# Three weight bits by way of ScalarE, and fewer idle products ahead of the first batch

## The chip, the cores and the metric

One Trainium2 chip, one of its cores. The metric is the time of one execution on the device in microseconds, as the median of several runs. The engines of the core are PE (TensorE, the matmuls), DVE (VectorE), ACT (ScalarE), POOL (GpSimd) and SP (SyncE, which issues most transfers); 16 DMA engines move data between the memory and the core.

## The reference, cut to what matters

Windowed causal attention with a distance bias over 8 batches of 8 heads, 576 positions and 64 dimensions, and behind it a network with a maximum of three linear maps.

```python
scores = scale * np.matmul(q, k.transpose(0, 1, 3, 2))
...
mask = (rel >= 0) & (rel < window)          # window = 128
scores = np.where(mask, scores + bias[None], -1000000000.0)
...
attn = attn / (np.sum(attn, axis=-1, keepdims=True) + 1e-09)
return np.matmul(attn, v).astype(np.float32)
...
x = np.ascontiguousarray(attn_out.transpose(0, 2, 1, 3)).reshape(B * S, H * D)
...
h = np.maximum(np.maximum(x @ w1, x @ w2), x @ w3)     # x 4608 x 512, w 512 x 768
return (h @ w_out).astype(np.float32)                  # w_out 768 x 512
```

The four weight matrices come as float64. The kernel takes them as 64-bit words and makes the float32 words on the chip.

## The kernel before, in words

**Layout.** The attention runs in steps: a task is a batch and a pair of heads, and a step is one block of 128 query rows of a task (five blocks, the last of 64 rows). A step has score products on PE (L563), a select and a bias with a row minimum on DVE, the exponential on ACT with its sum, a normalisation, transposes on PE (L671), masks on POOL (L700, L704) and the mixing with V on PE (L727, L759, later L782). The network's products go in units of six or nine matmuls of 128 x 288: those of the first batch by `plain_unit` (L1072), those of the other seven batches by `unit` and `multiply` (L1173), with fewer products per unit by a Strassen-like scheme. The attention of batch b+1 stands between the units of batch b.

**Weights.** `preparing` walks the 12 weight groups in `A_ORDER`. For each, `fetch` issues two loads of 512 KB (float64 halves, L138), `convert` turns each half into float32 words (24 calls in all), and `part` splits these into a high and a low fp32r part: a copy on ACT, then a subtraction on DVE (`halve`), for group after group of tiles `wt`, `ow`, `hs`, `xs`. The float32 words also go out to memory (L157) for the sums of the second batch, and the split parts to `keep` (L308, L295).

**Convert.** A float64 is a low word `lw` and a high word `hw`. The float32 word is sign and top exponent bit of `hw`, then 29 further bits of `hw` moved up by three, then the three top bits of `lw`. Three DVE instructions over 128 x 512 words do it: L146 moves and masks `hw` into a scratch tile `xt` (one buffer), L149 moves `lw` down by 29 and joins it into `xt`, L154 joins the top two bits of `hw` and writes the result over the first half of the loaded tile.

**Products that nothing reads.** `busy` puts bf16 matmuls of 128 x 512 on PE (L501), out of a constant tile into a PSUM bank that nobody reads; each is tied behind the matmul before it. `BUSY` holds how many follow what: eight at the start, eight after each of the first two score calls (`next`), five after each later score call (`s`), two after each transposing call (`t`), none after mixing (`x`). `plain_x(0)`, the split of the first batch's first half, ends this for good. The trace holds 73 weight loads of L501: 8, 16, 7 x 5 and 7 x 2.

**Order.** Up to the end of the first batch's units (`fix`) the framework's scheduler lays out each engine's order when the program is compiled, so an edit can reorder that part. Behind `fix`, PE, DVE and ACT keep the order that the kernel's own planner wrote (`job`, `issue`, `reach`). Each engine executes its instructions in order; the DMA queue of SP too.

Of the kernel before, what the change touches and what calls it, by code (L numbers as in the profile page):

```python
# [10 lines left out]
I32 = mybir.dt.int32  # L11
BF16 = mybir.dt.bfloat16
U32 = mybir.dt.uint32
AF = mybir.ActivationFunctionType
ALU = mybir.AluOpType
PSUM = bass.MemoryType.PSUM
# [2 lines left out]
LOAD_I = 1  # L19
LAG_T, LAG_X, LAG_X0 = 4, 6, 6  # L20
FOLLOW = 64
BUSY = {'start': 8, 'next': 8, 's': 5, 't': 2, 'x': 0}
GROUPS = (1, 4)
SHIFT = (0, 2, 4)
O_PACE = 0.285
# [5 lines left out]
def attention_maxout_kernel(  # L31
# [11 lines left out]
    nc = tc.nc  # L43
# [36 lines left out]
    nc.vector.memset(warm, 0.0)  # L80
    nc.scalar.activation(warm, warm, AF.Exp)
    ident = const.tile([P, P], F32, name="ident")
# [4 lines left out]
        out=prev, in_=prev, pattern=[[1, P]], compare_op=ALU.is_gt, fill=0.0,  # L87
# [3 lines left out]
    bias = const.tile([P, H, P], mybir.dt.bfloat16, name="bias")  # L91
# [5 lines left out]
    def slopes(hp):  # L97
        for h in (2 * hp, 2 * hp + 1):
            nc.scalar.activation(bias[:, h, :], dist, AF.Copy, scale=-8.0 * 2.0 ** (-8.0 * (h + 1) / H))
        nc.gpsimd.affine_select(  # L100
# [25 lines left out]
    raws = {}  # L126
# [11 lines left out]
            nc.sync.dma_start(raws[g, j], w_all[g, j].bitcast(I32))  # L138

    def convert(g, j):  # L140
        both = raws[g, j].bitcast(U32).rearrange("p (n w) -> p n w", w=2)
        lw, hw = both[:, :, 0], both[:, :, 1]


        u = xk_p.tile([P, 2, C], F32, name="xt").rearrange("p a c -> p (a c)")[:, :DM].bitcast(U32)
        nc.vector.tensor_scalar(  # L146
            out=u, in0=hw, scalar1=3, scalar2=0x3FFFFFFF, op0=ALU.logical_shift_left, op1=ALU.bitwise_and
        )
        nc.vector.scalar_tensor_tensor(  # L149
            out=u, in0=lw, scalar=29, in1=u, op0=ALU.logical_shift_right, op1=ALU.bitwise_or  # L150
        )

        out = raws[g, j][:, :DM]
        nc.vector.scalar_tensor_tensor(  # L154
            out=out.bitcast(U32), in0=hw, scalar=0xC0000000, in1=u, op0=ALU.bitwise_and, op1=ALU.bitwise_or
        )
        nc.sync.dma_start(  # L157
            w32[g][:, 1:3] if j else w32[g][:, ::3], out.bitcast(F32).rearrange("p (i w) -> p i w", w=W),
        )
# [47 lines left out]
    def job(engine, ns, slack, what, r=(), w=()):  # L207
        if not fixed:
            what()
            return  # L210
        j = Job(engine, ns, clock["pe"] + slack, what, r, w)
        for k in w:
            wrote[k] = j
        for k in r:
            read.setdefault(k, []).append(j)
        jobs.append(j)
# [210 lines left out]
    def preparing():  # L427
        fetch(A_ORDER[0])
        fetch(A_ORDER[1])
        for n, g in enumerate(A_ORDER):  # L430
            for j in range(2):
                convert(g, j)
                yield
            while AHEAD <= g < 9 and (g - 3 if AHEAD == 3 else g % 3, "plain") not in used:
                yield True
            for c in range(2):
                part(g, c)
                yield
            if n + 2 < 5:
                fetch(A_ORDER[n + 2])  # L440
            elif n + 2 == 5:
                for x in range(5, 5 + 4-1):
                    fetch(A_ORDER[x])
            elif n + 4 < NG:
                fetch(A_ORDER[n + 4])
# [50 lines left out]
    def busy(what):  # L496
        if idle[0] == "over":
            return
        ps = ps_m.tile([P, 512], F32, name="ps_m2")
        for _ in range(BUSY[what]):  # L500
            ins = nc.tensor.matmul(  # L501
# [87 lines left out]
    def score(t, i):  # L589
# [35 lines left out]
        def exponential(j):  # L625
            act.activation(
                p[:n, j], shifted[j][:n], AF.Exp, bias=st[:n, 0, h, j:j + 1], scale=-1.0,
                accum_out=st[:n, 1, h, j:j + 1],
# [20 lines left out]
    def normalise(t, i):  # L649
        n = rows[i]  # L650
        st, two = stats[t, i]
        for a, p in enumerate(two):
# [5 lines left out]
            for j in range(2):  # L658
                job("act", 293, 6000, partial(
                    act.activation, p[:n, j], p[:n, j], AF.Copy, scale=st[:n, 2, a, j:j + 1],  # L660
                ), r=[("st", t, i)], w=[("p", t, i - len(two) + 1 + a, j)])
# [546 lines left out]
    for t, (b, hp) in enumerate(tasks):  # L1208
        for i in range(NB):
            s = place_of[t, i] + shift[b]  # L1210
# [31 lines left out]
            g = next(e for e in GROUPS if e >= i)  # L1242
# [92 lines left out]
```

## Time and profile before

| what | before |
| --- | --- |
| runs | 747.1, 749.12, 747.11 us, median 747.11 |
| profiled execution | 748.33 us, of which 746.6 us are the span from the first to the last instruction |
| instructions | 20349 |
| PE busy | 738.4 us (99%) |
| DVE busy | 559.3 us (75%) |
| ACT busy | 496.0 us (66%) |
| POOL busy | 169.7 us (23%) |
| mean granted clock of PE | 0.999 |

Busy times overlap between engines. The ends of matmuls are modelled, so PE counts as busy in short waits too. 1.7 us of the profiled execution lie outside the span, and it took 1.22 us more than the median.

### The profile page before, as it was taken

How to read it: one execution, taken by the hardware profiler on the slowest of the kernel's cores; microseconds unless marked ns; L12 is line 12 of the kernel's file. 1: busy time of each engine (PE TensorE's matmuls, PEld its weight loads, DVE VectorE, ACT ScalarE, POOL GpSimd, SP SyncE). 2: the span in 40 equal slices, each digit the busy share in tenths (PEclk: the TensorE clock that was granted, in tenths of full speed). 3: DMA queues.
4: the chain of work that ended last, by engine and by line, in shares of the span. 5: the costliest groups of instructions: out<-in, count | busy, mean ns of one | idle time of the engine just before them, and what ended most of it. 6: DMA issues, size and time to landing. Idle time of an engine off the chain costs nothing.

```text
span 746.6 us, 20349 instructions
## 1 busy us (share of the span) xinstructions
PE 738.4 (99%) x7468; PEld 681.1 (91%) x7473; DVE 559.3 (75%) x1921; ACT 496.0 (66%) x1698; POOL 169.7 (23%) x371
## 2 busy tenths in 40 slices
PE   9999999999999999999999999999999999999998
PEld 4487888999999999999999999999999999999998
DVE  6989998959999477866679476684777756683663
ACT  5776886868887677665677676585776756552332
POOL 2431222012132232212322122221322123301100
PEclk9999999999999999999999999999999999999999
DMA  8799986969985688837896488856888379985631
GB/s 293 263 311 317 327 278 203 311 214 316 368 280 192 216 294 299 269 121 241 309 307 223 147 270 304 276 180 217 283 303 277 121 234 310 299 311 177 233 118 64
DMA packets 59091, 188.10 MB, mean 252 GB/s; under 512 B 6256, under 2 KB 21616, under 8 KB 52336
## 3 DMA queue, kind: packets, MB, share of 16 engines
q0 software_dynamic: 14976, 95.43, 38.8%
q1 hardware_dynamic: 43872, 91.31, 35.8%
q8 instruction: 59, 0.97, 0.5%
q14 instruction: 40, 0.33, 0.2%
q10 hardware_dynamic: 144, 0.07, 0.0%
HBM read 154.53 MB, written 32.24 MB: 250 GB/s over the span
## 4 chain that ended last, share of the span: by engine, by line
PE 86%; DVE 8%; DMA 3%; ACT 2%; issue 1%; SPq 0%; POOL 0%; DVEq 0%; ACTq 0%; POOLq 0%
PE ps_m L1173 57%; PE ps_m L1072 6%; PE ps_s L563 6%; PE pt L671 6%; PE ps_x L782 5%; PE ps_m L501 2%; DVE hq L174 1%; DMA keep<-wt 1%; PE pt L1173 1%; DVE wt L174 1%; ACT p L174 1%; DVE hs L174 1%; PE ps_x L759 1%; DMA hs<-in_w_all 1%; DMA wt<-keep 1%
## 5 line engine op out<-in xcount | busy, mean ns | idle before, releaser
L1173 PE MATMUL ps_m<-xs,wt 128*128 128x288 f32 x2562 | 357.5, 297 | 0.6 <-DVE t L174 0.4
L1173 PEld LDWEIGHTS ps_m<-xs,wt 128*128 128x128 f32 x2562 | 344.1, 188 | 2.2 <-DVE t L174 0.6
L700 POOL TENSOR_SCALAR_AFFINE_SELECT pp<-pr 128x256 f32<-128x256 f32 (+1 forms) x128 | 61.3, 479 | 352.1 <-ACT pr L174 328.4
L174 ACT COPY t<-ps_m 128x288 f32<-128x288 f32 x245 | 96.2, 393 | 67.4 <-PE ps_m L1173 65.1
L174 ACT ACTIVATE p<-s,st 128x128 f32<-128x128 f32 (+1 forms) x320 | 127.4, 400 | 18.9 <-DVE st L174 17.8
L174 DVE TENSOR_TENSOR t<-ps_m,t 128x288 f32<-128x288 f32 x164 | 73.8, 451 | 61.2 <-PE ps_m L1173 43.1
L1173 PE MATMUL ps_m<-hs,ow 128*128 128x288 f32 x774 | 109.5, 297 | 0.1
L174 ACT ACTIVATE p<-p,st 128x128 f32<-128x128 f32 (+1 forms) x296 | 103.3, 399 | 6.2 <-DVE st L174 5.6
L1173 PEld LDWEIGHTS ps_m<-hs,ow 128*128 128x128 f32 x774 | 104.1, 188 | 1.1 <-ACT t L174 0.3
L488 POOL DMA_DIRECT2D wt<-keep x104 | 56.2, 540 | 188.2 <-PE ps_m L1173 184.7
L174 DVE CUSTOM_DVE_ANT_0 s<-ps_s,bias 128x128 f32<-128x128 f32 (+1 forms) x300 | 75.2, 282 | 16.2 <-PE ps_x L782 8.1
L174 ACT COPY pr<-pt 128x256 f32<-128x256 f32 (+2 forms) x98 | 38.3, 399 | 66.4 <-PE pt L671 66.4
L174 ACT CAST hs<-hq 128x288 fp32r<-128x288 f32 x117 | 49.9, 433 | 45.6 <-DVE hq L174 45.5
L174 DVE COPY_PREDICATED ps_s<-prev,ps_s 128x256 f32<-128x256 uint8 x120 | 50.7, 422 | 31.8 <-PE ps_s L563 30.2
L563 PE MATMUL ps_s<-qk 64*64 64x192 f32 (+1 forms) x1052 | 62.2, 317 | 0.1
L782 PE MATMUL ps_x<-pp,v 64*64 64x64 f32 (+1 forms) x1632 | 61.8, 250 | 0.0
L174 ACT ACTIVATION_READ_ACCUMULATOR p<-s,st 128x1 f32 (+1 forms) x320 | 61.6, 192 | 0.0
L174 DVE TENSOR_TENSOR hq<-t,hq 128x288 f32<-128x288 f32 x126 | 57.8, 463 | 2.1
L704 POOL TENSOR_SCALAR_AFFINE_SELECT pp<-pr 128x256 f32<-128x256 f32 (+1 forms) x128 | 57.2, 447 | 5.6 <-PE ps_x L727 5.5
L174 DVE TENSOR_TENSOR hs<-hq,hs 128x288 fp32r<-128x288 f32 x117 | 52.3, 453 | 5.9 <-ACT hs L174 5.3
L671 PE MATMUL pt<-ident,p 128*128 128x128 f32 (+1 forms) x320 | 54.8, 281 | 0.4 <-ACT p L174 0.4
L782 PEld LDWEIGHTS ps_x<-pp,v 64*64 64x64 f32 x1632 | 46.1, 132 | 8.9 <-issue 8.3
(101 smaller groups left out, 861.7 us busy)
## 6 DMA issues: line engine op xcount, KB each, us to landing
wt<-keep POOLq DMA_DIRECT2D x52, 1024.0 KB, 7.6
wt<-keep POOLq DMA_DIRECT2D x52, 768.0 KB, 5.8
qk<-in_qk SPq DMA_DIRECT2D x28, 576.0 KB, 5.9
hs<-in_w_all SPq DMA_DIRECT2D x20, 512.0 KB, 6.2
outT<-t SPq DMA_DIRECT2D x64, 144.0 KB, 1.8
v<-in_v SPq DMA_DIRECT2D x28, 320.0 KB, 6.4
keep<-wt SPq DMA_DIRECT2D x30, 256.0 KB, 4.0
wt<-keep SPq DMA_DIRECT2D x27, 256.0 KB, 3.9
```

The source lines that it names most:

```text
L174: return lambda *a, **k: pe(getattr(self.engine, name)(*a, **k))
L488: nc.gpsimd.dma_start(wts[n, a], keep[n % 9][a])
L501: ins = nc.tensor.matmul(ps, lhsT=words[:, :P], rhs=words[:, 2 * C - 512:], start=True, stop=True, skip_group_check=True,)
L563: ins = nc.tensor.matmul(ps[j][d:d + D, o:o + k1 - k0], lhsT=qkt[t][j * D:(j + 1) * D, 0, q0:q0 + D], rhs=qkt[t][j * D:(j + 1) * D, 1, k0:k1],
L671: ins = nc.tensor.transpose(out=pt[:, a, j, :n], in_=p[:n, j], identity=ident[:n, :n])
L700: nc.gpsimd.affine_select(out=pp[t, i - 1][:, :, 1, :n], in_=x[:, a, :, :n], pattern=[[0, 2], [-1, n]], compare_op=ALU.is_gt, fill=0.0, ba ...
L704: nc.gpsimd.affine_select(out=pp[t, i][:n, :, 0, :n], in_=x[:n, a, :, :n], pattern=[[0, 2], [1, n]], compare_op=ALU.is_ge, fill=0.0, base= ...
L759: pe(nc.tensor.matmul(x[j * D:(j + 1) * D, c:c + e - a], lhsT=vv[:n, i, j * D:(j + 1) * D], rhs=w[:n, j].rearrange("p a b -> p (a b)")[:, ...
L782: ins = nc.tensor.matmul(x[j * D:(j + 1) * D, q0:q0 + e * D], lhsT=vt[t][ks, i, j * D:(j + 1) * D], rhs=pp[t, i][ks, j, a:a + e, qs * D:(q ...
L1072: pe(nc.tensor.matmul(ps, lhsT=lt, rhs=rt, start=m == 0 and c == 0, stop=m == len(pairs) - 1, skip_group_check=True,))
L1173: pe(nc.tensor.matmul(part_of[n, root(k)], lhsT=lt, rhs=rt, start=first and i == 0 and k in (0, 1, 4), stop=last and i == len(pairs) - 1, ...
```

## The change

In `convert`, L149 goes. In its place ACT reads byte 3 of each 8-byte word (the top byte of `lw`), multiplies by 1/32 with a bias that makes the rounding a rounding down, and writes the value 0 to 7 into byte 4 (the lowest byte of `hw`). The last DVE instruction takes these three bits with a wider mask. In `BUSY`, `s` falls from 5 to 2 and `t` from 2 to 0.

```diff
+U8 = mybir.dt.uint8
...
-BUSY = {'start': 8, 'next': 8, 's': 5, 't': 2, 'x': 0}
+BUSY = {'start': 8, 'next': 8, 's': 2, 't': 0, 'x': 0}
...
     def convert(g, j):
-        both = raws[g, j].bitcast(U32).rearrange("p (n w) -> p n w", w=2)
-        lw, hw = both[:, :, 0], both[:, :, 1]
-
+        hw = raws[g, j].bitcast(U32).rearrange("p (n w) -> p n w", w=2)[:, :, 1]
+        octets = raws[g, j].bitcast(U8).rearrange("p (n w) -> p n w", w=8)
...
-        nc.vector.scalar_tensor_tensor(
-            out=u, in0=lw, scalar=29, in1=u, op0=ALU.logical_shift_right, op1=ALU.bitwise_or
-        )
+        nc.scalar.activation(octets[:, :, 4], octets[:, :, 3], AF.Copy, scale=1 / 32, bias=-15.5 / 32)
...
-            out=out.bitcast(U32), in0=hw, scalar=0xC0000000, in1=u, op0=ALU.bitwise_and, op1=ALU.bitwise_or
+            out=out.bitcast(U32), in0=hw, scalar=0xC0000007, in1=u, op0=ALU.bitwise_and, op1=ALU.bitwise_or
```

## Rows read from the trace of the kernel before

**Rows 1.** The page: busy time of each engine; then the last chain by engine.

```profile
PE 738.4 (99%) x7468; PEld 681.1 (91%) x7473; DVE 559.3 (75%) x1921; ACT 496.0 (66%) x1698; POOL 169.7 (23%) x371
...
PE 86%; DVE 8%; DMA 3%; ACT 2%; issue 1%; SPq 0%; POOL 0%; DVEq 0%; ACTq 0%; POOLq 0%
```

**Rows 2.** Busy time by stretch: length, each engine with count, clock, DMA share, GB/s.

```profile
10.00:40.00 30.00, 29.51 (x228) 15.60 (x232) 29.02 (x124) 22.55 (x83) 11.29 (x20) 1.00 0.89 306
40.00:88.00 48.00, 46.44 (x414) 39.99 (x417) 45.34 (x154) 34.15 (x123) 9.98 (x20) 1.00 0.93 318
88.00:153.00 65.00, 64.51 (x578) 57.17 (x579) 59.28 (x202) 52.40 (x177) 12.89 (x29) 1.00 0.79 264
153.00:660.00 507.00, 506.00 (x5579) 482.06 (x5578) 372.42 (x1308) 349.83 (x1219) 127.16 (x281) 1.00 0.77 257
```

**Rows 3.** Chain that ended last, 0 to 10 us: start, length, what.

```profile
1.35 3.60 PE ps_m L501 x8
...
5.65 1.83 PE ps_m L501 x8
```

**Rows 4.** The same chain, 10 to 42 us: shares by line, and one piece.

```profile
by line: PE ps_m L501 31.0%; PE ps_x L727 14.5%; PE ps_m L563 13.0%; PE pt L671 13.0%; PE ps_s L563 10.3%; PE ps_m L1072 6.3%; ACT p L174 2.8%; issue 2.4%; DVE xt L149 1.8%; DVE xt L146 1.4%; DVE st L174 1.1%; DVE p L174 1.1%; DVE s L174 0.
...
12.52 1.19 PE ps_m L501 x5
```

**Rows 5.** The same chain, 40 to 88 us, by line.

```profile
by line: DMA hs<-in_w_all 12.3%; ACT p L174 10.8%; issue 8.7%; DVE xt L149 8.1%; PE ps_m L1072 7.1%; DVE wt L174 7.0%; DVE xt L146 5.8%; DVE hq L174 5.7%; DVE ow L174 5.5%; DVE hs L174 4.7%; DVE s L174 4.6%; DVE hs L154 4.0%; DVE ps_s L174 
```

**Rows 6.** The same chain, 88 to 130 us, by line, and one piece.

```profile
by line: PE ps_m L1072 63.7%; PE ps_x L759 15.4%; PE ps_s L563 10.8%; PE pt L671 10.5%
...
89.38 4.00 PE ps_m L1072 x30
```

**Rows 7.** Instruction groups, 10 to 153 us: count, busy us, mean ns, idle before.

```profile
L149 DVE SCALAR_TENSOR_TENSOR xt<-hs,xt 128x512 uint32<-128x512 uint32 x20 | 14.2, 711 | 0.0
...
L174 ACT CAST wt<-hs 128x512 fp32r<-128x512 f32 x12 | 7.3, 618 | 0.4 <-DVE hs L154 0.2
```

**Rows 8.** L149 alone by stretch: length, DVE busy with count, clock, DMA.

```profile
10.00:40.00 30.00, 4.59 (x6) 1.00 0.89 306
40.00:88.00 48.00, 7.15 (x11) 1.00 0.93 318
88.00:153.00 65.00, 5.20 (x8) 1.00 0.79 264
```

**Rows 9.** Waits, 10 to 153 us: total us, times, longest.

```profile
ACT p L174 <- DVE st L174: 14.0, 18, 1.7
...
DVE xt L146 <- DMA hs<-in_w_all: 1.9, 2, 1.7
...
DVE xs L174 <- ACT xs L174: 1.6, 2, 1.2
...
DVE hs L174 <- ACT hs L174: 1.0, 2, 0.5
```

**Rows 10.** Timeline, 43 to 45.5 us, DVE and ACT: start, length, engine, line.

```profile
43.58 0.68 DVE L149 SCALAR_TENSOR_TENSOR xt<-hs,xt 128x512 uint32<-128x512 uint32 x1
...
43.95 0.62 ACT L174 CAST wt<-hs 128x512 fp32r<-128x512 f32 x1
...
44.30 0.69 DVE L154 SCALAR_TENSOR_TENSOR hs<-hs,xt 128x512 uint32<-128x512 uint32 x1
44.47 0.70 ACT L174 ACTIVATE p<-p,st 64x128 f32<-64x128 f32 x2
44.91 0.89 DVE L174 TENSOR_TENSOR wt<-hs,wt 128x512 fp32r<-128x512 f32 x1
```

**Rows 11.** Busy time in two short stretches, columns as in the second group.

```profile
64.00:67.60 3.60, 2.76 (x35) 2.23 (x33) 3.60 (x10) 2.09 (x9) 0.00 (x0) 1.00 1.03 386
745.00:746.60 1.60, 0.00 (x0) 0.00 (x0) 0.00 (x0) 0.00 (x0) 0.00 (x0) 0.69 0.11 40
```

**Rows 12.** L501 alone: PE and its weight loads, 10 to 40 us.

```profile
10.00:40.00 30.00, 12.53 (x46) 4.13 (x49) 1.00 0.89 306
```

## The prediction

> **What bounds the kernel now.** I read the page first. PE is busy 99% of the span, and the last chain runs through PE for 86% of it [rows 1]. That says who sets the time in general; it doesn't say so for the part that is edited, and PE counts as busy in short waits. So I cut the span by stretches next [rows 2]. From 153 us on nothing is edited: there are no converts and no idle products, PE is busy 506 of 507 us, and the order is fixed. Whatever the change does, it does by moving the moment at which that part begins. The edited part is the first 153 us, and there I asked the chain, stretch by stretch.
>
> From 10 to 40 us (stretch I, the first three blocks of all four tasks) the chain is on PE, but 31.0% of it is L501, products that nothing reads [rows 4]. DVE is at the same time busy 29.02 of 30 us, or 96.7% [rows 2]: attention work mixed with the first converts. Two engines are full at once, one of them in part with filler. From 40 to 88 us (stretch II) the chain goes through DVE, ACT and one load of a weight half; L149 alone holds 8.1% of it [rows 5]. DVE is busy 45.34 of 48 us (94.5%). From 88 to 153 us (stretch III) the chain is PE up to 130 us, 63.7% of it the units' products at 4.00 us for 30 of them, 0.133 us each [rows 6], and PE is busy 64.51 of 65 us.
>
> **The products, part by part.** 35 of L501 go: three after each of seven score calls and both after each of seven transposing calls. Five of them take 1.19 us of the chain, 0.238 us each [rows 4], so 35 x 0.238 = 8.3 us of PE, all of it in stretch I, which holds all 49 of the later ones [rows 12]. 14 stay. Behind each removed one stand real products in PE's queue, so these start earlier. That helps as far as DVE and ACT can follow.
>
> **The convert.** L149 goes 24 times: 4.59 us in stretch I (6 of them), 7.15 us in II (11), 5.20 us in III (8, one shared at the border), 16.94 us of DVE [rows 8]. The three kept bits come from L154's wider mask, which costs nothing more: the same instruction with another constant, 0.69 us [rows 10]. ACT gets 24 new instructions over 128 x 512 bytes at a step of 8 bytes. The trace has no such form. The nearest is ACT's cast over 128 x 512, 0.618 us [rows 7]. The lower bound is 0.52 us, since ACT began its next instruction 0.52 us after the cast that I followed [rows 10]; the upper one is 1.2 us, twice the cast, if single bytes at a step are slow. I take 0.62, since the count of elements is the same, and since L149 read its words at a step of 8 bytes too and took no longer than L154 [rows 10]. That is 6 x 0.618 = 3.7 us in I, 6.8 us in II and 4.9 us in III.
>
> The convert now leaves DVE and comes back: L146, then ACT, then L154, and the scratch tile has one buffer, so the second half's L146 waits for the first half's L154. On DVE's queue selects, row minima and subtractions stand behind a waiting L154; on ACT the exponentials stand behind the new instruction. The same crossing exists already: each split is a copy on ACT and then a subtraction on DVE. In the whole edited part DVE waited for ACT in two rows only, 1.6 us and 1.0 us, and not once for the 12 casts of `wt`, since the scheduler puts other work between [rows 7, 9]. In the one convert that I followed, DVE had the next instruction at hand at each step [rows 10]. So I take 0.05 us for each of 24 crossings, 1.2 us, with 0 and 1.2 us each (the longest wait in those rows) as bounds. It fits inside what DVE saves. ACT's own waits for DVE, 14.0 us in 18 times [rows 9], should shrink, since DVE is less loaded.
>
> **The sum.** Stretch I: DVE falls to 24.4 us, PE to 29.5 - 8.3 = 21.2 us, ACT rises to 22.55 + 3.7 = 26.3 us and is now the fullest. If the fullest engine can be filled as DVE is today, 96.7%, the stretch takes 26.3 / 0.967 = 27.15 us: **-2.85 us**. Stretch II: ACT comes to 34.15 + 6.8 = 40.95 us, at today's 94.5% a stretch of 43.35 us, or -4.65. PE allows less. By its busy time (46.44 us, at the 99.2% of stretch III) it could be only 1.2 us shorter. By counting it could be 4.4: 230 products at 0.133 us are 30.6 us, and the attention between them, 36.3% of 42 us for some seven pairs of steps in the PE chain [rows 6], is about 13 us for the six pairs here. Between 1.2 and 4.4 I take **-2.2 us**, nearer the lower one, since ACT would be 89% full there, DMA is at 0.93 [rows 2], and one weight load already stands on the chain. Stretch III: PE has 0.5 us to give; **-0.4 us**. Together -5.45 us. The profiled execution took 748.33 us (746.6 of span), which gives 742.9; it was 1.22 us above the median, so I forecast 741.7 us.
>
> **The clock.** Do the filler products carry the clock? The first eight take 3.60 us, 0.45 each, the next eight 1.83 us, 0.23 each: PE began at 1.2 GHz and was at 2.4 GHz from about 5 us [rows 3]. Those 16, and the eight behind the second score call, stay. The leanest stretch I found at the full clock has PE busy 2.76 of 3.60 us, 77% [rows 11]. Stretch I after the change: 29.51 - 12.53 + 14 x 0.272 = 20.8 of 27.15 us, 77% as well [rows 2, 12]. So the rows just reach to where I need them, on the mean and not for its leanest moments. The only fall in the trace comes behind the last product, with PE idle [rows 11].
> The Trainium skill, "TensorE: Matmul & The Clock Gate", section "What's actually happening", says that the slow clock is the rule and activity lifts it, and its "Part 4: PE-mode transpose" says that transposes don't count as such activity in the same way. Transposes are a good part of what stays in stretch I, so by that page the clock could fall there and the time would be that of the clock rival below; no row here shows a fall under load.
>
> **The rivals.**
> *More comes (10%).* PE's whole 4.4 us in II, and stretch I as short as DVE allows, 24.4 / 0.967 = 25.3 us because converts slide behind it: -4.7 - 4.4 - 0.5 = -9.6, 737.5 us. For it: 31% filler in the chain. Against: ACT.
> *Nothing comes (20%).* The freed DVE time falls where PE or the transfers bind anyway. DMA is at 0.89 and 0.93 in I and II [rows 2], and the layout that the scheduler draws anew may have as many small holes. Then 745 to 748 us, say 746.5. For it: the load of a weight half on the chain [rows 5]. Against: DVE waited for such loads only twice, 1.9 us [rows 9].
> *The crossing costs more than the instruction (10%).* L154 stands at the head of DVE's queue and waits for an ACT that is 87% to 97% full. The point is 16.94 / 24 = 0.71 us of wait per convert; at 1.2 us it is 28.8 - 16.9 = 11.9 us more on DVE, 17 of 24 parts of it in I and II where DVE is full: +8.4, 755.5 us. For it: ACT becomes the fullest engine. Against: today's crossings cost almost nothing.
> *The clock falls in stretch I (12%).* Real PE work there is 30 - 49 x 0.238 = 18.3 us, with the 14 kept 21.6 us. At 1.2 GHz for a share f of it PE needs 21.6 (1 + f) us; above f = 0.26 it binds, at f = 0.51 all gain is gone. Half the time: 747 us (5%). All the time: 43.2 us against 27.15, 758 us (7%).
>
> **How the numbers follow.** The forecast itself holds 48%, and with its bounds (II from -1.2 to -4.4, I from -1.5 to -4) it runs from 738.5 to 744.8 us. 0.3%, about what a measurement of this kernel can tell from no change, is 2.2 us. Faster: 48 + 10 = 58%. Same: 20% and the half-fallen clock, 25%. Slower: the crossing and the fully fallen clock, 17%. A range of 735.5 to 751 us leaves out about 5% below and 13% above.
>
> **What would show it.** Right: units of the second batch (L1173) begin near 148 us instead of 153.4; no L149; 24 ACT instructions of about 0.62 us; L501 with 38 loads; ACT the fullest of DVE and ACT between 10 and 88 us; the clock at 1.00 throughout; waits of DVE's L154 for ACT under 2 us in total. Wrong: the new ACT instruction well above 0.7 us; L154 with several microseconds of wait for ACT; products of L563 or L671 twice as long between 10 and 40 us; or a start of L1173 that has moved while the end has not, which would mean that the second batch waits for something else.

## The result and the profile after

The changed kernel takes 756.58 us (median of five runs, 756.28 to 758.07) against 747.1 us for the kernel before (five runs, 746.5 to 749.12): 1.0127 times, with a 95% interval of 1.011 to 1.0145. It became 9.5 us slower; the forecast was 5.45 us faster. The profiled execution took 756.58 us, 754.5 us of it span. In the changed kernel's line numbers the ACT instruction is L149, the last DVE instruction of `convert` L152, the attention's helper L172; `busy` is L499, scores L561, transposes L669, POOL's masks L698 and L702, mixing L725 and L757, the first batch's products L1070, those of the others L1171.

The page, busy time of each engine and the last chain by engine:

```profile
PE 740.3 (98%) x7438; PEld 679.4 (90%) x7438; DVE 546.4 (72%) x1897; ACT 520.9 (69%) x1722; POOL 166.8 (22%) x371
...
PE 79%; ACT 8%; DVE 7%; DMA 2%; issue 2%; POOL 0%; SPq 0%; ACTq 0%; DVEq 0%; POOLq 0%
```

Beside [rows 1], the share of PE in the chain fell from 86% to 79%, and ACT's rose from 2% to 8%. So the next question is where ACT stands in the chain. Busy time by stretch, the columns of [rows 2]; the last two stretches follow the later border:

```profile
10.00:40.00 30.00, 28.75 (x216) 14.34 (x215) 24.45 (x124) 25.64 (x89) 9.21 (x20) 1.00 0.82 275
40.00:88.00 48.00, 45.83 (x372) 37.47 (x372) 36.64 (x124) 44.79 (x126) 8.45 (x18) 1.00 0.81 275
88.00:128.00 40.00, 34.46 (x312) 28.58 (x310) 30.68 (x116) 37.62 (x114) 7.79 (x18) 1.00 0.83 279
128.00:162.00 34.00, 34.00 (x298) 31.20 (x298) 29.85 (x98) 26.68 (x86) 6.14 (x14) 1.00 0.81 271
162.00:668.00 506.00, 505.36 (x5574) 481.45 (x5574) 372.29 (x1306) 349.73 (x1216) 126.78 (x279) 1.00 0.77 257
```

Where DVE was full [rows 2], ACT is now: 44.79 of 48 us, then 37.62 of 40. From 88 to 128 us PE is busy 34.46 of 40 us, where it had half a microsecond of 65 to give before. The clock is at 1.00 throughout, and the last row shows the same work at the same pace as before. So the loss is complete when the second batch begins. The products' first and last starts tell when that is, first the changed kernel:

```profile
L1070 PE MATMUL ps_m<-xs,wt x336: 288/295/482, 35.8 to 137.9; 128*128 128x288 f32 x168
...
L1171 PE MATMUL ps_m<-xs,wt x2562: 288/295/402, 161.8 to 738.2; 128*128 128x288 f32 x198
```

and the kernel before:

```profile
L1072 PE MATMUL ps_m<-xs,wt x336: 288/295/479, 39.1 to 128.6; 128*128 128x288 f32 x168
...
L1173 PE MATMUL ps_m<-xs,wt x2562: 288/295/404, 153.6 to 730.3; 128*128 128x288 f32 x198
```

The first batch's products begin 3.3 us earlier (35.8 against 39.1), and the second batch begins 8.2 us later (161.8 against 153.6). Some 11 us are lost in between. Another form of the first batch's products tells where, again the changed kernel first:

```profile
L1070 PE MATMUL ps_m<-xs,ow x96: 288/295/400, 55.1 to 95.2; 128*128 128x288 f32 x96
...
L1072 PE MATMUL ps_m<-xs,ow x96: 288/295/398, 54.1 to 89.9; 128*128 128x288 f32 x96
```

The last of them starts 5.3 us late (95.2 against 89.9), so most of the loss falls between 40 and 95 us. The new instruction, its durations as shortest, median and longest, and who waited for it:

```profile
L149 ACT ACTIVATE hs<-hs x20: 1323/1362/1390, 13.6 to 124.6; 128x512 uint8<-128x512 uint8 x20
L149 ACT ACTIVATE xs<-xs x4: 1359/1372/1377, 65.2 to 121.6; 128x512 uint8<-128x512 uint8 x4
...
  DVE hs L152: 13.7, 17
  DVE xs L152: 2.1, 4
```

It takes 1.36 us, not 0.62, and DVE's L152 waits 15.8 us for it in 21 of 24 converts. The same instruction by stretch (length, ACT busy, clock, DMA):

```profile
10.00:40.00 30.00, 5.36 (x4) 1.00 0.82 275
40.00:88.00 48.00, 16.40 (x12) 1.00 0.81 275
88.00:162.00 74.00, 10.87 (x9) 1.00 0.82 275
```

Together it is 32.6 us of ACT. DVE was rid of 16.94 us [rows 8] and stands waiting for 15.8 us of it. The chain by line, 40 to 88 and 88 to 130 us:

```profile
by line: ACT hs L149 19.9%; ACT p L172 18.5%; DMA v<-in_v 14.8%; PE ps_m L1070 7.0%; issue 6.8%; PE ps_x L725 4.4%; ACT pr L172 4.3%; ACT hq L172 4.1%; ACT ow L172 3.4%; ACT wt L172 3.3%; PE ps_s L561 3.2%; DVE hs L152 1.9%; DVE hq L172 1.9
...
by line: ACT p L172 23.5%; ACT hs L149 17.8%; DMA hs<-in_w_all 9.6%; issue 8.7%; ACT xs L149 6.3%; PE ps_m L1070 3.8%; DVE xs L152 3.3%; ACT hs L172 3.1%; ACT wt L172 2.7%; DVE s L172 2.7%; ACT ow L172 2.5%; DVE ps_s L172 2.0%; ACT hq L172 
```

Against [rows 5, 6]: from 40 to 88 us the chain went over loads, ACT and DVE, and now L149 and the exponentials behind it hold 38%; from 88 to 130 us it was PE's alone, and now ACT leads there too. One convert, ACT from one answer of the timeline and DVE from another (in brackets the idle time before):

```profile
13.62 1.33 ACT L149 ACTIVATE hs<-hs 128x512 uint8<-128x512 uint8 x1
...
14.98 0.69 DVE L152 SCALAR_TENSOR_TENSOR hs<-hs,xt 128x512 uint32<-128x512 uint32 x1 [0.57 <-ACT hs L149]
```

### The profile page after: what moved, and what is told of

It reads as the page before. It is cut to its first block, busy times and chain, and to the rows that moved or that the text cites. A ratio compares the mean times of both kernels' runs of the same rounds, so it can differ in the third digit from the quotient of the medians.

```text
span 754.5 us, 20282 instructions
## 1 busy us (share of the span) xinstructions
PE 740.3 (98%) x7438; PEld 679.4 (90%) x7438; DVE 546.4 (72%) x1897; ACT 520.9 (69%) x1722; POOL 166.8 (22%) x371
## 3 DMA queue, kind: packets, MB, share of 16 engines
q0 software_dynamic: 14976, 95.43, 38.5%
## 4 chain that ended last, share of the span: by engine, by line
PE 79%; ACT 8%; DVE 7%; DMA 2%; issue 2%; POOL 0%; SPq 0%; ACTq 0%; DVEq 0%; POOLq 0%
PE ps_m L1171 55%; PE ps_s L561 5%; PE pt L669 5%; PE ps_x L780 5%; PE ps_m L1070 4%; ACT p L172 3%; ACT hs L149 2%; DVE hq L172 2%; PE ps_m L499 1%; DVE hs L172 1%; PE pt L1171 1%; DVE t L172 1%; DMA v<-in_v 1%; PE ps_x L725 1%; DVE wt L172 1%
## 5 line engine op out<-in xcount | busy, mean ns | idle before, releaser
L1171 PE MATMUL ps_m<-xs,wt 128*128 128x288 f32 x2562 | 357.5, 297 | 0.2
L1171 PEld LDWEIGHTS ps_m<-xs,wt 128*128 128x128 f32 x2562 | 344.1, 188 | 1.7 <-DVE hq L172 0.3
L172 ACT COPY t<-ps_m 128x288 f32<-128x288 f32 x245 | 96.5, 395 | 66.3 <-PE ps_m L1171 64.4
L698 POOL TENSOR_SCALAR_AFFINE_SELECT pp<-pr 128x256 f32<-128x256 f32 (+1 forms) x128 | 60.2, 471 | 366.2 <-ACT pr L172 355.5
L172 ACT ACTIVATE p<-s,st 128x128 f32<-128x128 f32 (+1 forms) x320 | 127.5, 401 | 11.6 <-DVE st L172 10.3
L172 DVE TENSOR_TENSOR t<-ps_m,t 128x288 f32<-128x288 f32 x164 | 73.8, 451 | 61.2 <-PE ps_m L1171 43.0
L1171 PE MATMUL ps_m<-hs,ow 128*128 128x288 f32 x774 | 109.6, 297 | 0.1
L1171 PEld LDWEIGHTS ps_m<-hs,ow 128*128 128x128 f32 x774 | 104.2, 188 | 1.2 <-ACT t L172 0.3
L172 ACT ACTIVATE p<-p,st 128x128 f32<-128x128 f32 (+1 forms) x296 | 103.1, 399 | 2.9 <-DVE st L172 2.5
L172 DVE CUSTOM_DVE_ANT_0 s<-ps_s,bias 128x128 f32<-128x128 f32 (+1 forms) x300 | 75.5, 282 | 17.1 <-PE ps_x L780 8.1
L172 ACT COPY pr<-pt 128x256 f32<-128x256 f32 (+2 forms) x98 | 39.0, 406 | 64.8 <-PE pt L669 64.7
L172 ACT CAST hs<-hq 128x288 fp32r<-128x288 f32 x117 | 50.0, 435 | 42.0 <-DVE hq L172 42.0
L172 DVE COPY_PREDICATED ps_s<-prev,ps_s 128x256 f32<-128x256 uint8 x120 | 50.7, 423 | 32.1 <-PE ps_s L561 30.5
L561 PE MATMUL ps_s<-qk 64*64 64x192 f32 (+1 forms) x1052 | 64.8, 320 | 4.0 <-DVE st L172 4.0
L172 ACT ACTIVATION_READ_ACCUMULATOR p<-s,st 128x1 f32 (+1 forms) x320 | 62.0, 194 | 0.0
L669 PE MATMUL pt<-ident,p 128*128 128x128 f32 (+1 forms) x320 | 57.2, 283 | 2.7 <-ACT p L172 2.7
L172 DVE TENSOR_TENSOR hq<-t,hq 128x288 f32<-128x288 f32 x126 | 57.8, 462 | 2.1
L172 DVE TENSOR_TENSOR hs<-hq,hs 128x288 fp32r<-128x288 f32 x117 | 52.2, 452 | 6.3 <-ACT hs L172 5.6
L702 POOL TENSOR_SCALAR_AFFINE_SELECT pp<-pr 128x256 f32<-128x256 f32 (+1 forms) x128 | 55.7, 436 | 2.0 <-PE ps_x L725 1.9
```

The source lines that it names most:

```text
L172: return lambda *a, **k: pe(getattr(self.engine, name)(*a, **k))
L561: ins = nc.tensor.matmul(ps[j][d:d + D, o:o + k1 - k0], lhsT=qkt[t][j * D:(j + 1) * D, 0, q0:q0 + D], rhs=qkt[t][j * D:(j + 1) * D, 1, k0:k1],
L669: ins = nc.tensor.transpose(out=pt[:, a, j, :n], in_=p[:n, j], identity=ident[:n, :n])
L698: nc.gpsimd.affine_select(out=pp[t, i - 1][:, :, 1, :n], in_=x[:, a, :, :n], pattern=[[0, 2], [-1, n]], compare_op=ALU.is_gt, fill=0.0, ba ...
L702: nc.gpsimd.affine_select(out=pp[t, i][:n, :, 0, :n], in_=x[:n, a, :, :n], pattern=[[0, 2], [1, n]], compare_op=ALU.is_ge, fill=0.0, base= ...
L1171: pe(nc.tensor.matmul(part_of[n, root(k)], lhsT=lt, rhs=rt, start=first and i == 0 and k in (0, 1, 4), stop=last and i == len(pairs) - 1, ...
```

## The experiments

Three theories could tell the same story. **Length**: ACT is full because the instruction takes 1.36 us. **Hand-over**: any step over ACT in the middle of the convert costs, however short. **Order**: the scheduler lays out the first batch anew after any edit, and its new order is worse. The kernels cut L149's length, take it away, undo the products, or tie the order. "Tied" means that each engine's instructions, up to the first batch's end, are held in the compiled order of the kernel before; only the kept products of `busy` and the new instruction find their own place. The clock, a fourth, is answered under the rivals below.

| run | median, us | ratio, 95% interval | first batch's products from | second batch from |
| --- | --- | --- | --- | --- |
| e1_products_alone | 751.72 | 1.0068 [1.0055, 1.0081] | 39.3 | 157.0 |
| e2_byte_alone | 759.92 | 1.018 [1.0163, 1.0197] | 42.1 | 165.0 |
| e3_byte_half_length | 752.1 | 1.0068 [1.0054, 1.0081] | 35.9 | 156.1 |
| e5_byte_tiny | 751.85 | 1.0072 [1.0048, 1.0096] | 37.0 | 155.0 |
| e6_products_in_old_order | 746.25 | 0.9991 [0.998, 1.0002] | 38.2 | 153.3 |
| e7_load_on_act_alone | 754.68 | 1.0104 [1.009, 1.0118] | 40.5 | 160.5 |
| e8_whole_words | 758.13 | 1.0136 [1.0105, 1.0166] | 43.9 | 163.5 |
| e9_drop_in_old_order | 743.73 | 0.9962 [0.9949, 0.9974] | 38.5 | 149.3 |
| e10_change_in_old_order | 765.22 | 1.0253 [1.0237, 1.0269] | 41.1 | 170.8 |
| e11_byte_on_pool | 754.73 | 1.0112 [1.0086, 1.0138] | 39.9 | 160.0 |
| e12_tiny_in_old_order | 746.23 | 0.9993 [0.9977, 1.001] | 36.3 | 152.2 |
| e13_drop_redrawn | 753.28 | 1.0084 [1.0056, 1.0112] | 38.2 | 160.1 |
| e14_only_t | 749.71 | 1.0044 [1.0029, 1.0059] | 38.6 | 154.3 |
| e15_only_s | 750.7 | 1.005 [1.0032, 1.0069] | 38.5 | 155.7 |
| e16_pin_dve | 759.29 | 1.0164 [1.0118, 1.021] | 39.5 | 160.4 |
| e17_pin_pe | 746.69 | 0.9993 [0.9978, 1.0007] | 38.1 | 152.2 |
| e18_change_pin_pe | 758.36 | 1.0155 [1.0125, 1.0185] | 40.7 | 163.0 |

The kernel before had a median between 746.7 and 747.3 us beside these runs. The two last columns are from each run's one profiled execution.

**e1: the products alone.** Only `BUSY` is edited; the converts are the old ones.

```diff
-BUSY = {'start': 8, 'next': 8, 's': 5, 't': 2, 'x': 0}
+BUSY = {'start': 8, 'next': 8, 's': 2, 't': 0, 'x': 0}
```

> Only the numbers in BUSY change (s 5 to 2, t 2 to 0); the convert stays on DVE. Theory 1 (the byte instruction on ACT took 1.36 us in place of 0.62 and filled ACT) and theory 2 (going to ACT and back is the cost, whatever its length): this part is not what made the kernel slower, so 738 to 747.5 us, by the sum of the forecast about 745. Theory 3 (the removed products, or the new order that their removal brings, did it): 752 us or more.

It is 4.6 us slower, and its first products don't start earlier. A wait is new, that of PE's mixing products for POOL's masks. In e1, 10 to 60 us (total, times, longest):

```profile
PEld ps_x L727 <- POOL pp L700: 5.3, 10, 1.5
...
PEld ps_x L727 <- POOL pp L704: 2.3, 4, 0.9
PE ps_x L727 <- POOL pp L700: 1.8, 4, 1.2
```

and all that there was of it in the kernel before:

```profile
PEld ps_x L727 <- POOL pp L700: 0.4, 1, 0.4
```

Removing work that nothing reads can turn PE's time into waiting, but is by itself no reason for a slower kernel. That the order had moved was a guess here; e6 tries it.

**e2: the convert alone**, with the products at 5 and 2 as before.

```diff
-BUSY = {'start': 8, 'next': 8, 's': 2, 't': 0, 'x': 0}
+BUSY = {'start': 8, 'next': 8, 's': 5, 't': 2, 'x': 0}
```

> Only the convert changes; BUSY keeps 5 and 2. Theories 1 and 2: 755 us or more, ACT 20 us busier, waits of L152 for ACT of about 15 us. Theory 3: within 1.5 us of 747.

It is 12.8 us slower, 3.3 us more than the whole change: the convert alone, with the order free, is enough for the loss.

**e3 and e5: a shorter instruction.** The change, with ACT on the first 256 (e3) or 8 (e5) words of each half.

```diff
-nc.scalar.activation(octets[:, :, 4], octets[:, :, 3], ...)
+nc.scalar.activation(octets[:, :256, 4], octets[:, :256, 3], ...)   # e5: :8
```

> The changed kernel, but the ACT instruction works on 256 of the 512 words only (the other 256 words keep wrong lowest three bits: that part is left out). Its length should come to about 0.77 us, near the 0.62 that the forecast had assumed. Theory 1: the time falls to 741 to 749 us and the waits of L152 for ACT fall below 6 us. Theory 2: the crossing is still there 24 times, so 754 us or more.

> The changed kernel with the ACT instruction on 8 of the 512 words (the other 504 words keep wrong lowest three bits: that part is left out). The crossing from DVE to ACT and back is there 24 times, the ACT time is nearly gone (about 0.2 us each), and DVE is relieved as in the changed kernel. Theory 1 (length of the ACT instruction): 738 to 745 us, by the three lengths 1.36, 0.77 and 0.2 a line. Theory 2 (the crossing): 751 us or more. Theory 3 (the order that the scheduler draws anew): 747 to 752, as with the products alone.

```profile
L149 ACT ACTIVATE hs<-hs x20: 760/784/808, 13.5 to 117.8; 128x256 uint8<-128x256 uint8 x20
...
  DVE hs L152: 6.3, 12
  DVE xs L152: 1.4, 2
```

That is e3: 0.78 us an instruction, and 7.7 us of waits instead of 15.8. It gains 4.5 us on the whole change; at 752.1 us it lies in neither of my two ranges. But e5, at 0.22 us with 2.3 us of waits, gains no more, and both stay some 5 us above the kernel before. So length explains about half of the loss in these orders. Whether the other half is the hand-over's or the order's, these two don't tell: 751.85 us lies in the ranges of both theories. e5 is also the least even of the kernels: 749.96 and 750.27 us in two executions with a mean clock of 1.000 (the granted clock over the whole span), 753.43 and 754.11 us in two with 0.998 and 0.995.

**e4: the form of the instruction.** The kernel before, with a row of ACT instructions behind its end that nothing reads (one execution, taken for the durations alone).

```diff
+for _ in range(3):
+    nc.scalar.activation(bytes_out[:, :, 4], bytes_in[:, :, 3], ...)   # L1312, as in the change
+    nc.scalar.activation(flat_out[:, :512], bytes_in[:, :, 3], ...)    # L1313, written side by side
+    nc.scalar.activation(bytes_out[:, :, 4], flat_in[:, :512], ...)    # L1314, read side by side
+    ...
```

> The kernel before with 12 forms of the ACT copy over 128 x 512 elements, three times each, behind all other work, on two tiles of zeros; they differ in type and step of what is read and written. If writing or reading single bytes at a step of 8 bytes is what takes 1.36 us, the forms with words or with bytes side by side take 0.62 us and the split between reading and writing shows in the mixed forms. If the scale and bias in the instruction or the byte type itself cost it, the forms with bytes side by side take 1.36 us as well. The time of the kernel only grows by the added work, some 40 us.

The timeline of ACT (start, duration, line, types of output and input):

```profile
753.43 1.33 ACT L1312 ACTIVATE hs<-hs 128x512 uint8<-128x512 uint8 x1
754.79 0.65 ACT L1313 ACTIVATE hs<-hs 128x512 uint8<-128x512 uint8 x1
755.48 1.33 ACT L1314 ACTIVATE hs<-hs 128x512 uint8<-128x512 uint8 x1
756.84 0.63 ACT L1315 ACTIVATE hs<-hs 128x512 uint8<-128x512 uint8 x1
...
758.19 1.34 ACT L1317 ACTIVATE hs<-hs 128x512 uint8<-128x512 f32 x1
759.56 1.33 ACT L1318 ACTIVATE hs<-hs 128x512 uint16<-128x512 uint16 x1
760.93 0.65 ACT L1319 ACTIVATE hs<-hs 128x512 f32<-128x512 f32 x1
```

L1315 reads and writes bytes side by side, L1317 reads float32 words side by side and writes bytes at a step of 8, L1318 has 16-bit values and L1319 32-bit words at a step of 8 bytes on both sides. Reading at a step costs nothing (L1313, 0.65), nor do bytes as such (L1315, 0.63), nor 32-bit words written at a step (L1319, 0.65). Single bytes or 16-bit values *written* at a step take twice as long: 1.33 us.

**e8: whole words written.** ACT writes the three bits as a 32-bit word over `lw`, and L146 joins them in.

```diff
+low = raws[g, j].rearrange("p (n w) -> p n w", w=2)[:, :, 0]
+nc.scalar.activation(low, octets[:, :, 3], AF.Copy, scale=1 / 32, bias=-15.5 / 32)
...
-nc.vector.tensor_scalar(
-    out=u, in0=hw, scalar1=3, scalar2=0x3FFFFFFF, op0=ALU.logical_shift_left, op1=ALU.bitwise_and
+nc.vector.scalar_tensor_tensor(
+    out=u, in0=hw, scalar=3, in1=low.bitcast(U32), op0=ALU.logical_shift_left, op1=ALU.bitwise_or
...
-nc.scalar.activation(octets[:, :, 4], octets[:, :, 3], AF.Copy, scale=1 / 32, bias=-15.5 / 32)
...
-    out=out.bitcast(U32), in0=hw, scalar=0xC0000007, in1=u, op0=ALU.bitwise_and, op1=ALU.bitwise_or
+    out=out.bitcast(U32), in0=hw, scalar=0x3FFFFFFF, in1=u, op0=ALU.bitwise_or, op1=ALU.bitwise_and
```

> A mended form of the change: ACT writes the three bits as a whole 32-bit word over the low word (0.65 us by the forms measured before), straight behind the load, and two DVE instructions join them (0.68 us each; the mask uses that all weights lie between 2^-127 and 2 in size). BUSY stays at 2 and 0. One way from ACT to DVE is left of the crossing. Theory 1: 740 to 748 us. Theory 2: at most half of the loss of e3, some 748 to 750. Theory 3: anything from 744 to 752, by the order.

I expected a cure and got 758.13 us. The first stretch, in the columns of [rows 2]:

```profile
10.00:40.00 30.00, 25.03 (x164) 10.39 (x164) 20.09 (x97) 19.64 (x70) 6.41 (x15) 0.89 0.70 236
```

All engines do less there, and the granted clock is 0.89. ACT, now first in the convert, waits 5.8 us for loads. A short instruction at another place of the convert brings another order. What that order costs is mixed with the clock: the profile is that of the slowest of four executions. Three with a mean clock of 0.992 or 0.993 took 758.08 to 759.83 us, and the one with 1.000 took 753.23 us, 3.4 us less than the changed kernel. One execution is too few to say that the shorter instruction helped.

**e6: the products in the old order.** e1 with every engine and queue tied.

```diff
+for engine, order in ORDER.items():                # positions in the compiled order of before
+    for x, y in zip(order, order[1:]):
+        tc.add_manual_dep(made[engine][y], made[engine][x].name, ...)   # order alone, no semaphore
```

> As with the products alone (BUSY 2 and 0, convert on DVE), but every engine's instructions of the first batch and both DMA queues are tied into the order that they have in the kernel before; only the kept idle products find places of their own. Theory 3 (the new order cost the 4.6 us): 743 to 748 us, not slower than before. If the removed products themselves cost the time, by the clock or by another way: 750 us or more, as with the products alone.

The 4.6 us are gone (0.9991, 0.998 to 1.0002). So the loss in e1 is the order's. But nothing is won either:

```profile
10.00:40.00 30.00, 25.13 (x200) 12.67 (x201) 29.05 (x128) 23.11 (x86) 12.39 (x20) 1.00 0.87 296
```

PE's busy time falls from 29.51 to 25.13 us, and DVE is still at 29.05: the freed time becomes waiting.

**e9: the relief alone.** Tied, products at 5 and 2, L149 of the kernel before left out and nothing in its place.

```diff
-nc.vector.scalar_tensor_tensor(
-    out=u, in0=lw, scalar=29, in1=u, op0=ALU.logical_shift_right, op1=ALU.bitwise_or
-)
```

> The order of the kernel before on every engine, its products (5 and 2) and no byte instruction at all: L149 is left out and with it the three lowest bits of each weight. This is the whole relief of DVE, 16.9 us of instructions, with no price. If DVE's fullness before 88 us holds the kernel up, as the forecast said, 738 to 744 us. If DVE is full only because converts fill its gaps, and the units wait for something else, 745.5 us or more.

It takes 743.73 us, 3.0 us less. This bounds what a free byte step would be worth in this order with the products kept:

```profile
10.00:40.00 30.00, 29.60 (x231) 15.67 (x227) 25.74 (x120) 22.95 (x86) 9.52 (x20) 1.00 0.90 304
40.00:88.00 48.00, 48.00 (x444) 42.43 (x443) 41.55 (x153) 37.24 (x135) 10.94 (x22) 1.00 0.97 337
```

PE is as full as before from 10 to 40 us, in part with products that nothing reads, and the first batch's products start at 38.5 us, hardly earlier. The gain comes behind 40 us, where PE is full and DMA at 0.97.

**e12: both parts, tied, with a tiny instruction.** The changed kernel, held in the old order as in e6, and

```diff
-nc.scalar.activation(octets[:, :, 4], octets[:, :, 3], ...)
+nc.scalar.activation(octets[:, :8, 4], octets[:, :8, 3], ...)
```

> The whole change in the order of the kernel before, with the ACT instruction on 8 of 512 words (the other 504 keep wrong lowest three bits: that part is left out). At this order L149 dropped without any ACT instruction gave -3.0 us and the full ACT instruction +18.5 us. If the length of the ACT instruction is what costs, 743 to 746 us. If the crossing costs by itself, 750 us or more.

The first products start at 36.3 us, 2.8 us earlier, the second batch at 152.2, only 1.4 us earlier, and the median, 746.23 us, is not to be told from before; it lies just above the range of the length theory. Its chain, 88 to 130 us, by line and one piece:

```profile
by line: DMA hs<-w 17.2%; ACT p L263 13.7%; PE ps_m L1162 11.4%; issue 9.1%; DVE hq L263 5.7%; DVE hs L263 5.4%; DVE wt L263 5.1%; DVE s L263 3.9%; DVE ps_s L263 3.4%; PE pt L761 3.0%; PE ps_x L849 2.8%; ACT hs L263 2.5%; DVE ow L263 2.5%; 
...
118.68 7.24 DMA hs<-w
```

In the kernel before that chain was PE's alone [rows 6]. A load of float32 words for the second batch's sums is new in it. But the load alone doesn't take the gain back, since e9, which kept 3.0 us, has it in its chain too:

```profile
by line: PE ps_m L1161 43.0%; DMA hs<-w 14.8%; PE ps_x L848 10.3%; PE pt L760 7.2%; PE ps_s L652 7.2%; DVE hs L261 5.4%; DVE ow L261 2.3%; DVE hq L261 1.9%; DVE s L261 1.9%; DVE ps_s L261 1.6%; DVE xt L261 1.5%; issue 1.4%; SPq L423 0.8%; D
...
116.78 6.20 DMA hs<-w
```

What differs is the time ahead of the load: there e9's chain is PE's, and e12's runs over ACT and DVE. And e12's last DVE instruction of the convert (L243) waits 9.7 us for ACT, though the instruction on ACT takes 0.22 us:

```profile
L240 ACT ACTIVATE hs<-hs x20: 204/218/230, 13.8 to 113.6; 128x8 uint8<-128x8 uint8 x20
...
  DVE hs L243: 9.1, 9
  DVE xs L243: 0.6, 1
```

That is a hand-over in an order that was made without one. So the hand-over may be what takes the gain back. The run that would settle it, L149 left out with the products at 2 and 0 and everything tied, is missing.

**e10: the whole change, tied.** Against e12:

```diff
-nc.scalar.activation(octets[:, :8, 4], octets[:, :8, 3], ...)
+nc.scalar.activation(octets[:, :, 4], octets[:, :, 3], ...)
```

> The whole change (byte on ACT, products 2 and 0), but all instructions that both kernels have stand in the order of the kernel before; only the 24 ACT instructions and the kept products find places of their own. If the 9.5 us are the new order's 4.6 and the ACT instruction's length, 749 to 753 us: the first part goes, the second stays. If the new order had been what made room for the ACT instruction, 756 us or more.

My 749 to 753 us fell: it took 765.22 us. L152's counterpart waits 23.3 us for ACT, 16 times, and the clock falls (two stretches, columns of [rows 2]):

```profile
  DVE hs L243: 21.6, 15
  DVE xs L243: 1.7, 1
...
18.70:22.00 3.30, 2.98 (x20) 1.66 (x20) 2.17 (x8) 2.96 (x8) 1.71 (x4) 0.50 0.84 264
...
10.00:40.00 30.00, 25.60 (x175) 12.20 (x176) 23.34 (x112) 24.22 (x82) 9.65 (x19) 0.83 0.80 276
```

Against e12, which differs in the instruction's length alone, it is 19 us slower. The changed kernel, with the same instruction in the scheduler's new order, is 8.6 us faster than this one, as my second case had it: the new order made room for the long instruction. The clock doesn't order the four executions: 764.96 and 765.0 us at a mean of 0.984 and 0.982, 765.44 and 766.33 us at 0.989 and 0.988.

**e7: load on ACT, without a hand-over.** The kernel before, with two byte instructions of 256 elements in each convert, into a half that nobody reads again.

```diff
+for x in range(2):
+    nc.scalar.activation(octets[:, :, 4 + x], octets[:, :, 3], AF.Copy, scale=1 / 32, bias=-15.5 / 32)
```

> The kernel before with its three DVE instructions and its products, and 24 times two more ACT copies of 256 bytes at a step of 8 bytes, 0.77 us each, in the dead second half of the loaded tile; nothing on DVE waits for them. If a fuller ACT (about 36 us more before 120 us) costs by itself, 752 us or more. If only the wait of DVE for ACT costs, within 2.5 us of 747.

It is 7.4 us slower, with no instruction waiting for the new ones. ACT is busy 45.28 of 48 us from 40 to 88 us. Its order was free, so part of this may be the order's: the run agrees with the length theory and doesn't prove it.

**e11: the byte on POOL** (tied, products at 2 and 0).

```diff
-nc.scalar.activation(octets[:, :, 4], octets[:, :, 3], AF.Copy, scale=1 / 32, bias=-15.5 / 32)
+nc.gpsimd.tensor_scalar(out=octets[:, :, 4], in0=octets[:, :, 3], scalar1=1 / 32, scalar2=-15.5 / 32, ...)
```

> As the kernel before this one in the list, but POOL, busy a fifth of the time, makes the byte instead of ACT. If its instruction takes about 1 us and POOL's masks are not late, it has the relief of DVE without the load on ACT: between the time with L149 dropped and 3 us more. If POOL takes 3 us or more per instruction, or holds up DVE's port to the memory, 750 us or more.

It takes 754.73 us, 8.0 more. POOL needs as long as ACT for it:

```profile
L240 POOL TENSOR_SCALAR hs<-hs x20: 1324/1365/1800, 14.5 to 122.2; 128x512 uint8<-128x512 uint8 x20
```

The last DVE instruction waits 10.5 us for it, 10 times, and the clock is at 0.94 and 0.96 in the first two stretches. The two executions with a mean clock of 0.998 took 752.85 and 753.29 us, those with 0.995 and 0.992 756.18 and 757.78 us. Of the two reasons that I had named for 750 us or more, 3 us per instruction is not the case, and the port wasn't looked at. An engine that is 23% busy [rows 1] is not for that a free place.

**e13: the relief alone, order free** (e9's edit, products at 2 and 0, untied). **e14 and e15: one of the two numbers alone**, `t` from 2 to 0 or `s` from 5 to 2.

```diff
-BUSY = {'start': 8, 'next': 8, 's': 5, 't': 2, 'x': 0}
+BUSY = {'start': 8, 'next': 8, 's': 5, 't': 0, 'x': 0}   # e14
+BUSY = {'start': 8, 'next': 8, 's': 2, 't': 2, 'x': 0}   # e15
```

> L149 left out (with it the three lowest bits), no ACT instruction, products 2 and 0, and the scheduler free to lay out the first batch. If the order costs the 4.6 us of the run with 8 words, this one too is at 749 to 753 us. If the crossing cost them, 742 to 745 us, as with L149 dropped in the old order.

> Only the products behind the transposes go (s stays 5, t 2 to 0), order free. If any redrawing of the order costs about as much, 749 to 753 us. If the loss lies in the other number, 746 to 748.

> Only the products behind the score calls fall from 5 to 2 (t stays 2), order free. If any redrawing of the order costs about as much, 749 to 753 us. If the redrawn order is a matter of chance, anywhere from 744 to 753, not in step with the number of products.

e13 has less work on DVE *and* on PE, none more on ACT and no hand-over, and is 6.2 us slower (752.0 and 752.55 us in its two executions with a mean clock of 1.000, so the clock isn't the reason for most of it). The two small edits cost 2.7 and 3.7 us. All the untied kernels without a long ACT instruction (e1, e3, e5, e13, e14, e15) lie 2.7 to 6.2 us above the kernel before, whatever was edited. For e1 that it is the order is shown by e6; for the others it is the reading that fits all of them.

**e16 and e17: which engine's order.** e1 with DVE's order alone, or PE's alone, tied.

```diff
-ORDER = {'Activation': [...], 'Pool': [...], 'SP': [...], 'PE': [...], 'DVE': [...]}   # e6
+ORDER = {'DVE': [...]}   # e16
+ORDER = {'PE': [...]}    # e17
```

> Products alone (2 and 0), with DVE's instructions of the first batch tied into the order of the kernel before and all other engines and queues free. If DVE's order (where the converts stand between the attention steps) carries the 4.6 us, the time goes back to 745 to 748 us. If PE's order carries them, 750 us or more.

> The same with PE's order tied and DVE, ACT and the queues free. If PE's order carries the loss, 745 to 748 us; if DVE's, 750 us or more. If both fall to 745 to 748, one follows from the other and either is enough.

With PE's order held the loss is gone (0.9993), with DVE's alone it grows to 12 us (757.48 us in the fastest execution; the two slowest have a mean clock of 0.99). So in e1 it is PE's order that carries it. The waits of the mixing products for masks, 10 to 60 us, added up over their rows, are 9.9 us in e1, 11.5 in e16, 0.6 in e17 and 1.4 in e6; but in e14 and e15 they are 2.2 and 1.2 us and the time is lost all the same, so they are only part of it.

**e18: the whole change with PE's order alone tied.** Against e10:

```diff
-ORDER = {'Activation': [...], 'Pool': [...], 'SP': [...], 'PE': [...], 'DVE': [...]}
+ORDER = {'PE': [...]}
```

> The whole change with PE's order of the first batch tied to that of the kernel before, everything else free. If order and length add up, about 5 us above before: 750 to 753 us. If PE's redrawn order had been the one that fits the longer ACT instruction, 756 us or more, as with the whole change free, or worse.

I expected 750 to 753 us and got 758.36. With the long instruction, PE's old order is no help: L152's counterpart still waits 15.4 us, 19 times, and the time is about that of the changed kernel with its order free. The two losses don't add; each order has to be judged with the instruction that it serves.

## Why the prediction was wrong

**The step that failed first is the price of the ACT instruction.** I took 0.62 us, from the cast of the same size [rows 7], and named 1.2 us as the upper bound "if single bytes at a step are slow". It took 1.36 us, above both. Nor had I carried that bound into the range. With 1.2 us my sum gives (22.55 + 6 x 1.2) / 0.967 = 30.8 us for stretch I and (34.15 + 11 x 1.2) / 0.945 = 50.1 us for II, 2.9 us slower in all, and my forecast's own range ended at 744.8 us (its stated bounds add up to 738.3 to 744.0). My argument was that L149 read its words at a step of 8 bytes at no cost; e4 shows that reading so is indeed free and *writing* narrow values so is not. Put into my own sum, 1.36 us turns it round: stretch I (22.55 + 6 x 1.36) / 0.967 = 31.8 us, +1.8; stretch II (34.15 + 11 x 1.36) / 0.945 = 52.0 us, +4.0; together 5.8 us slower instead of 5 faster. The sign is then right, but not the path. Stretch I came out 3.3 us shorter; only four of the 24 instructions fell into it, where the sum had six, and the whole loss lies behind it. The waits were mis-sized too: I took 1.2 us for the 24 crossings, and DVE waited 15.8 us. Measured from e5 to the whole change, the length costs 4.7 us with a free order.
The Trainium skill, "ScalarE: Activation LUTs", section "What ACT_TABLE_LOAD costs", gives an instruction with immediate scale and bias, at a rate that it states for fp32 and bf16, 186 ns + 0.833 ns an element, by which 512 elements are about 613 ns, an estimate. The rows agree for values written side by side or as whole words (0.63 and 0.65 us) and differ for the form used here: from e3 to the whole change 256 elements more take 1.362 - 0.784 = 0.578 us, 2.3 ns each.

**The second is that the sum had no term for the order.** I let a redrawn order in only as small holes under "Nothing comes". In the six free kernels without the long instruction the time is 2.7 to 6.2 us longer, and in the one case that was taken apart (e1, e6, e16, e17) it is PE's order. So even the assumed price would not have given the forecast: e3, at 0.78 us, is 5.0 us slower than before. With the long instruction the sign turns: there the free order is 8.6 us better than the old one (e10).

**The sizes.** The relief of DVE was worth 3.0 us (1.9 to 3.8) with the products kept and nothing put on ACT (e9). The first products start 2.8 us earlier in e12 (forecast 2.85), where DVE and PE are relieved at once; relieved singly, they come 0.6 and 0.9 us earlier (e9 and e6). That two engines were full at once was the right reading of [rows 2, 4]. That e12 meets the number is in part luck, as its ACT instruction has 8 words, not the 512 of the sum. And the gain of I did not last to the end. The "Nothing comes" rival said 746.5 us, and e12 took 746.23; its reason, the transfers, isn't shown, since e9 has the same load in its chain and kept its gain.

**The rivals.** The crossing rival set its point at 0.71 us of wait per convert; it measured 15.8 / 24 = 0.66 us, just short, and 755.5 us was near the result. But the hand-over itself can't carry the 9.5 us: e12 has all 24 of them, 9.7 us of waits, and is not slower than before. It may not be free: e12 is some 2.3 us behind e9, which has none, by the ratios 0.9993 and 0.9962, and differs from it in the products too. What costs more is the length, 19 us from e12 to e10. That this works through a full ACT, and not only through DVE's longer waits, rests on e7, whose order was free: it is argued, not shown. The clock rival fell for the changed kernel (1.00 throughout). In other kernels' profiles the clock did dip: from 10 to 40 us 0.83 in e10, 0.89 in e8, 0.96 in e18, 0.94 in e11 and in e17, whose median is that of the kernel before; from 40 to 88 us 0.96 in e2, e13 and e16.

**What was right:** that all is decided before the second batch begins; that DVE falls to 24.4 us in stretch I (24.45, in part by luck, as fewer converts fell into it); that ACT becomes the fullest of the two; that the products can go at no cost, as long as the order stays (e6). Two small readings were off: DVE waited for ACT in a third row as well, 0.4 us, and 153.4 us was the start of the first batch's last product; the second batch began at 153.6.

**What stays open:** why PE's new orders are worse beyond the waits for masks; what takes e12's gain back; how much of e10's 19 us is its fallen clock; and how much of the time of e8, e11, e16 and e18, whose slower executions have the lower clock, is the clock's. How the loss of 9.5 us divides depends on the path. By one it is -0.8 us (e12), then 5.6 us for the free order (e5), then 4.7 us for the length; by the other -0.8 us (e12), then 19.0 us for the length (e10), then -8.6 us for the free order. Each free order is another draw, and the six free kernels above spread over some 3 us. So the length alone makes the kernel slower in the old order, far beyond the noise, what it does to the clock there included; with the free order its 4.7 us are not much above that spread, and a share of the order in the changed kernel is argued, not shown. No version here is measurably faster than the kernel before with all its bits.

## What to carry to other kernels

An instruction's price belongs to its form: measure it with the types and steps of its *output* before moving work onto an engine that is 71% busy there already. A compiled order is part of a tuned kernel, so an edit is tried with the order held as well as free; here the same edit gave 1.0068 and 0.9991. Two full engines relieved together moved the first stretch most, but the best time came with DVE relieved alone (e9): a gain in one stretch counts only as far as it reaches the part that follows.

## What the runs showed of the hardware

- ACT takes 1.33 us instead of 0.65 to write 128 x 512 values of 1 or 2 bytes at a step of 8 bytes, while 4-byte words at the same step cost nothing more (e4). POOL took 1.37 us for the same bytes (e11).
- PE's clock fell while PE worked. In e10 it was 0.50, which is the lower level of 1.2 GHz, from 18.7 to 22 us; in the 8.7 us before, at full clock, PE had been busy 7.03 us:

```profile
10.00:18.70 8.70, 7.03 (x59) 3.35 (x58) 6.30 (x32) 6.31 (x24) 1.71 (x4) 1.00 1.02 373
```

  In the kernel before the clock stayed at 1.00 while PE was busy 2.76 of 3.60 us [rows 11], a smaller share, so these rows don't tell what made it fall.
- A dip of the clock goes with a longer time in some kernels and not in others: e8 took 753.23 us at a mean of 1.000 and 758.08 to 759.83 us at 0.992 or 0.993, while in e10 the two with 0.982 and 0.984 took 765.0 and 764.96 us and the two with 0.989 and 0.988 no less, 765.44 and 766.33 us.
